# An attention, gated MLP and squared-ReLU MLP kernel: q and k transposed in memory, and a list scheduler in place of a table of times

## The chip, the cores and the metric

The kernel runs on one core of one Trainium2 chip. The metric is the device time of an execution in microseconds, the median of several runs. The five engines have queues of their own, each worked off in order: TensorE (PE; its loads of weights are PEld), VectorE (DVE), ScalarE (ACT), GpSimd (POOL) and SyncE (SP, which here only issues transfers). An instruction that has to wait for another engine holds up all that stands behind it in its queue.

## What is computed

```python
scores = scale * np.matmul(q, k.transpose(0, 1, 3, 2))          # B, H, S, D = 2, 8, 768, 64
is_global = pos[None, :] < int(n_global)                         # 8
is_local = (rel >= 0) & (rel < int(n_local))                     # 96
dist = np.where(is_global & ~is_local, float(n_local), np.abs(rel).astype(np.float32))
scores = scores - slopes[:, None, None] * dist[None, :, :]
scores = np.where(is_global | is_local, scores, -1000000000.0)
a = np.exp(scores - np.max(scores, axis=-1, keepdims=True))
x = np.matmul(a / (np.sum(a, axis=-1, keepdims=True) + 1e-09), v)   # to 1536 tokens x 512
...
xn = x / np.sqrt(np.mean(x * x, axis=-1, keepdims=True) + 1e-06) * rms_g
g = xn @ w_gate                                                  # 512 x 1536
x = g * (1.0 / (1.0 + np.exp(-g))) * (xn @ w_val) @ w_out        # 1536 x 512
...
r = np.maximum(x @ w_in, 0.0)                                    # 512 x 2048
return (s * (r * r) + b) @ w_out2                                # 2048 x 512
```

The weights of the MLPs are 64-bit floating point in memory and are converted in the kernel. All products are of 32-bit numbers split into a high and a low part: hi x hi, lo x hi and hi x lo are added up.

## The kernel before

A first branch (L993) tests that the mask has its known size and takes `fast_program` (L583); the other branch is not run here. A **unit** is a block of 128 queries of one batch; there are 12 (L576), in the order block 0 of both batches, block 1 of both, and so on. A unit sees 232 keys: 8 global ones, 96 before the block and its own 128 (for block 0 only its 128). It has two **groups** of four heads, 24 in all.

For each unit `emit_t` (L655) has PE transpose q and k (`transposes`, L225, recorded at L228) out of tiles that SP loads with 256-byte rows (`load_qk`, L609), splits them from PSUM into high and low parts (L689 to L694, L673, L676) on ScalarE and VectorE, and `shift` (L645, L652) moves the last 96 keys of the block before to the front of the window. `emit_s` (L706) makes the scores of a group (L721); VectorE adds the distances and finds the extreme value (L735), ScalarE makes the exponentials (L750), VectorE the reciprocal of the sums (L760, L761), GpSimd mostly normalizes (L762). `emit_p` transposes the weights (L782), ScalarE or VectorE copies them out of PSUM (L786, L788), `emit_x` multiplies with v (L807). `Mlp.finish` (L375) then norms a unit's 128 tokens: squares on ScalarE, their sum on VectorE (L381), two small products on PE (L384, L391), a power on GpSimd (L388), the scaling on VectorE (L395) and the split into `xyh` and `xyl` (L403 to L407).

An **item** is the gate and value product (24 matmuls) of one of the first four slices f of 128 hidden columns with 256 tokens (`hb`). Items are PE's filler in the attention stage (`gate_val`, L830); where there is none yet, `keep_warm` (L210, L215) puts matmuls without use there. Each weight goes through seven steps (`steps`, L298): magnitude (ScalarE, L304), floor (GpSimd as a rule, L307), shift and two merges (VectorE, L309 to L312), high part (ScalarE, L319), low part (GpSimd as a rule, L321). A ring of eight holds converted weights, three buffers the raw ones.

What orders the attention stage is the table `SCH` (L39): for each kind of step and each group a time, in units of a group, and for some the engine. Every step is put into a heap with its time (`at`, L603) and recorded when its time is the least (L886 to L888). After it `mlp.run` (L446) does the rest: first the items that are left, halves of one slice and 512 tokens together, then the other slices of gate and value, `w_out`, `w_in`, `w_out2`; weights are converted as it goes on.

Of the kernel before, what the change touches and what calls it, by code (L numbers as in the profile page):

```python
# [14 lines left out]
ALU = mybir.AluOpType  # L15
# [15 lines left out]
WIN = GLOB + PREV + 128  # L31
KA = GLOB + PREV
# [6 lines left out]
SCH = {  # L39
    "exp": [0.406, 0.27, -0.303, 0.212, 0.116, 0.271, 0.267, 0.276, 0.13, 0.198, 0.245, -0.017, 0.207, 0.102, 0.226, 0.093,  # L40
     0.229, 0.063, 0.093, 0.104, 0.446, 0.273, 0.395, 0.115],
    "nrm": [0.47, 0.057, 0.226, 0.329, 0.232, 0.292, 0.157, 0.111, -0.107, 0.33, 0.258, 0.244, 0.279, 0.33, 0.325, 0.292, -0.129,
     0.382, 0.399, 0.382, 0.957, 0.22, 0.706, 0.494],
    "nrmV": [1, 0, 0, 0, 0, 0, 0, 0, 0, 0, 1, 0, 0, 0, 0, 0, 0, 0, 0, 0, 0, 0, 0, 0],
    "cp": [[1.578, 1.356, 1.511, 1.695, 1.502, 1.722, 1.62, 1.606, 1.716, 1.318, 1.604, 1.565, 1.357, 1.884, 1.72, 1.721, 1.707,
      1.261, 1.519, 1.48, 2.115, 1.317, 1.296, 1.27],
     [1.809, 1.308, 1.802, 1.667, 1.543, 1.794, 1.284, 1.845, 1.968, 1.901, 1.643, 1.845, 1.845, 2.06, 1.994, 1.88, 2.012,
      1.646, 1.736, 0.894, 1.769, 1.457, 2.015, 0.921]],
    "cpV": [2, 3, 2, 2, 0, 0, 0, 0, 3, 0, 2, 0, 0, 1, 0, 1, 0, 3, 0, 1, 2, 1, 0, 0],
    "gv": [0.52, 0.511, 0.36, 0.367, 0.413, 0.069, 0.482, 0.489, 0.687, 0.535, 0.535, 0.54, 0.449, 0.497, 0.491, 0.465, 0.42,  # L50
     0.413, 0.49, 0.498, 0.644, 0.479, 0.444, 0.451, 0.522, 0.898, 0.79],
    "silu": [0.43, 0.084, -0.119, -0.292, -0.217, -0.528, -0.709, -0.095, -0.138, 0.033, 0.104, -0.177, 0.312, -0.094, 0.03,
     -0.37, 0.197, 0.105, 0.102, -0.062, 0.197, -0.17, 0.097, -0.107, 0.093, 0.07, -0.011],
    "mult": [0.092, 0.611, 0.115, -0.071, -0.311, 0.77, -0.266, 0.298, -0.118, 0.974, 0.112, 0.343, 0.223, 0.14, 0.14, 0.641,
     0.083, 0.654, 0.146, 0.822, 0.076, 0.322, -0.007, 0.811, 0.161, 0.297, -0.14],
    "dum": [4, 6, 5, 3, 0, 0, 0, 3, 7, 7],
    "maxV": [1, 0, 0, 1, 1, 0, 1, 0],
    "loV": [0, 1, 0, 1, 1, 0, 1, 0],
    "T": [-0.692, -1.029, -1.323, -1.024, -1.16, -0.983, -1.043, -0.991, -1.008, -1.263, -0.942, -1.184],
    "shift": [-2.152, -1.955, -2.004, -1.861, -1.935, -1.162, -1.655, -1.947, -1.543, -1.814, -1.669, -1.843],  # L60
    "fin": [[3.268, 3.837, 4.209, 4.21, 4.346, 4.403, 4.976, 4.977], [2.932, 3.306, 4.163, 4.164, 4.27, 4.428, 5.069, 5.12],
# [11 lines left out]
    "conv": [[0.47, 2.049, 2.05, 2.152, 3.896, 3.897], [1.905, 2.353, 3.218, 4.031, 4.064, 4.148],  # L73
# [3 lines left out]
    "mask": -2.172,  # L77
# [7 lines left out]
    "hiV": [0, 1, 0, 0, 0, 0, 0, 0, 0, 0, 0, 1],  # L85
    "shP": [1, 0, 0, 0, 0, 0, 1, 0, 0, 0, 1, 1],
    "top": [-0.042, 0.11, 0.089, 0.074, -0.522, 0.021, 0.095, 0.104, 0.013, -0.261, -0.145, -0.306, -0.167, -0.517, 0.067, 0.202,
     0.062, -0.044, 0.066, -0.509, 0.021, 0.117, 0.141, -0.043],
    "val": [0.768, 0.053, 0.09, -0.108, -0.135, -0.174, 0.09, -0.162, 0.011, -0.109, -0.112, -0.107, -0.234, 0.054, -0.052,
     -0.375, 0.032, 0.166, -0.671, -0.346, -0.661, 0.036, 0.348, 0.117, -0.029, 0.377, -0.348],  # L90
    "fe": [[1, 0], [0, 0], [1, 0], [1, 0], [1, 0], [0, 0], [0, 0], [1, 1], [1, 1], [1, 1], [0, 0], [0, 0]],
    "bmP": [0, 0, 0, 1, 0, 1, 1, 1],
}
SLOPES = [2.0 ** -(h + 1) for h in range(H)]
# [3 lines left out]
def kernel(  # L98
# [34 lines left out]
    nc.sync.dma_start(qn0, q[0, :, 0:128, :].rearrange("h t d -> t h d"))  # L133
    nc.scalar.dma_start(kn0, k[0, :, 0:128, :].rearrange("h t d -> t h d"))


    def distance(Dt, W, base, scr):
# [902 lines left out]
```

## Time and profile before

| | us |
|---|---|
| median of 3 runs | 703.92 (703.17 to 704.7) |
| the profiled execution | 703.05 |
| its span, from first to last instruction | 701.3 |
| PE busy | 672.8 |
| VectorE busy | 436.3 |
| ScalarE busy | 283.5 |
| GpSimd busy | 258.9 |

The span's mean granted TensorE clock is 0.98 of full speed. Busy time counts overlapping instructions of an engine once. A row of the timeline has the start, the time taken and the work; matmuls overlap, so what one costs PE is read from start to start. In the windows each engine's busy time stands in the order PE, PEld, DVE, ACT, POOL.

### The profile page before, as it was taken

The numbers are of one execution on the slowest core, as the hardware profiler recorded it, in microseconds if no ns is written. First come the engines' busy times: TensorE is split into PE (matmuls) and PEld (weight loads), VectorE is DVE, ScalarE is ACT, GpSimd is POOL, SyncE is SP. The second block draws the span as 40 slices with busy tenths as digits, with TensorE's granted clock in tenths as the row PEclk, the third lists the DMA queues.
The fourth block names the chain that finished last, engine by engine and source line by source line (L and its number), as shares of the span: only waits on it lengthen the run. The fifth ranks groups of instructions, "written<-read, shape, count | busy, mean of one in ns | idle before, by whom it ended". The sixth has DMA issues, their size and how long they took to land.

```text
span 701.3 us, 9949 instructions
## 1 busy us (share of the span) xinstructions
PE 672.8 (96%) x3707; PEld 562.6 (80%) x3707; DVE 436.3 (62%) x868; ACT 283.5 (40%) x611; POOL 258.9 (37%) x194
## 2 busy tenths in 40 slices
PE   7789999999999999999999999999999997999996
PEld 5578888989988888887888877888888875888885
DVE  6989897775577766778432379654544599322332
ACT  3766566654233322334332344433333454322321
POOL 1644454333356654566200066433333377000000
PEclk7869999999999999999999999999999999999999
DMA  7754543410032331223200023221122222100101
GB/s 169 160 118 114 120 103 76 99 45 1 8 114 90 93 117 61 91 90 108 75 0 1 0 88 120 66 89 60 61 64 80 68 92 89 61 1 0 61 1 65
DMA packets 64562, 51.11 MB, mean 73 GB/s; under 512 B 29624, under 2 KB 59384, under 8 KB 64504
## 3 DMA queue, kind: packets, MB, share of 16 engines
q1 hardware_dynamic: 63320, 50.11, 25.2%
q8 instruction: 31, 0.51, 0.3%
q10 hardware_dynamic: 1184, 0.26, 0.2%
q14 instruction: 27, 0.22, 0.1%
HBM read 47.22 MB, written 3.15 MB: 72 GB/s over the span
## 4 chain that ended last, share of the span: by engine, by line
PE 82%; DVE 6%; POOL 4%; ACT 3%; DMA 2%; issue 2%; SPq 0%; POOLq 0%; ACTq 0%; DVEq 0%
PE ps L223 24%; PE ps L222 24%; PE ps L221 24%; PE ps L782 2%; PE ps L807 2%; PE ps L721 2%; PE ps L228 1%; DMA raw_p<-in_moe_w_out_dram 1%; POOL u L307 1%; ACT t L750 1%; DMA side<-in_q_dram 1%; DVE u L309 1%; DVE u L310 1%; PE ps L391 1%; POOL t L762 1%
## 5 line engine op out<-in xcount | busy, mean ns | idle before, releaser
L307 POOL TENSOR_SCALAR u<-u 128x512 f32<-128x512 f32 x64 | 111.2, 1738 | 143.4 <-ACT u L304 143.4
L221 PE MATMUL ps<-xyh,hi_i 128*128 128x512 f32 x192 | 74.7, 389 | 0.0
L222 PE MATMUL ps<-xyl,hi_i 128*128 128x512 f32 x192 | 74.7, 389 | 0.0
L223 PE MATMUL ps<-xyh,lo_i 128*128 128x512 f32 x192 | 74.7, 389 | 0.0
L514 DVE SCALAR_TENSOR_TENSOR gt<-side,sb 128x512 f32<-128x512 f32 x48 | 38.5, 803 | 57.3 <-ACT side L513 57.3
L221 PE MATMUL ps<-xyh,hi_g 128*128 128x512 f32 (+1 forms) x188 | 65.3, 347 | 0.0
L221 PE MATMUL ps<-xyh,hi_v 128*128 128x512 f32 (+1 forms) x188 | 64.0, 340 | 0.0
L222 PE MATMUL ps<-xyl,hi_v 128*128 128x512 f32 (+1 forms) x188 | 63.8, 339 | 0.0
L223 PE MATMUL ps<-xyh,lo_v 128*128 128x512 f32 (+1 forms) x188 | 63.8, 339 | 0.0
L222 PE MATMUL ps<-xyl,hi_g 128*128 128x512 f32 (+1 forms) x188 | 63.7, 339 | 0.0
L223 PE MATMUL ps<-xyh,lo_g 128*128 128x512 f32 (+1 forms) x188 | 63.7, 339 | 0.0
L309 DVE TENSOR_SCALAR u<-u 128x512 int32<-128x512 int32 x68 | 61.4, 903 | 2.2 <-POOL u L307 2.1
L513 ACT ACTIVATE side<-ps 128x512 f32<-128x512 f32 x48 | 28.7, 598 | 76.7 <-PE ps L223 76.7
L762 POOL TENSOR_TENSOR t<-t,sm 128x928 f32<-128x928 f32 (+1 forms) x22 | 36.7, 1670 | 59.1 <-ACT xn L379 20.9
L428 ACT ACTIVATE side<-ps 128x512 f32<-128x512 f32 (+1 forms) x47 | 23.3, 497 | 86.5 <-PE ps L223 86.3
L750 ACT ACTIVATE t<-t,mn 128x232 f32<-128x232 f32 (+1 forms) x96 | 44.2, 463 | 16.0 <-DVE mn L735 15.9
L222 PEld LDWEIGHTS ps<-xyl,hi_i 128*128 128x128 f32 x192 | 36.0, 188 | 7.5
L223 PEld LDWEIGHTS ps<-xyh,lo_i 128*128 128x128 f32 x192 | 36.0, 188 | 7.5
L434 DVE TENSOR_TENSOR p<-side,ps 128x512 f32<-128x512 f32 (+1 forms) x47 | 26.3, 560 | 25.2 <-PE ps L223 24.9
L221 PEld LDWEIGHTS ps<-xyh,hi_i 128*128 128x128 f32 x192 | 36.0, 188 | 7.3
L429 DVE SCALAR_TENSOR_TENSOR side<-side,ps 128x512 f32<-128x512 f32 (+1 forms) x47 | 26.3, 559 | 23.7 <-ACT side L428 23.6
L223 PE MATMUL ps<-hi_p,ev 128*128 128x512 f32 x96 | 37.8, 394 | 2.5 <-DVE ev L521 2.5
(155 smaller groups left out, 1650.1 us busy)
## 6 DMA issues: line engine op xcount, KB each, us to landing
raw_i<-in_moe_w_in_dram SPq DMA_DIRECT2D x16, 512.0 KB, 4.0
raw_p<-in_moe_w_out_dram SPq DMA_DIRECT2D x16, 512.0 KB, 3.2
raw_g<-in_moe_w_gate_dram SPq DMA_DIRECT2D x12, 512.0 KB, 3.5
raw_v<-in_moe_w_val_dram SPq DMA_DIRECT2D x12, 512.0 KB
raw_o<-in_moe_w_out_dram SPq DMA_DIRECT2D x12, 512.0 KB, 3.3
vw<-in_v_dram SPq DMA_DIRECT2D x10, 448.0 KB, 4.4
out_dram<-o SPq DMA_DIRECT2D x12, 256.0 KB, 2.1
qn<-in_q_dram SPq DMA_DIRECT2D x11, 256.0 KB, 3.9
```

What stands on the lines that cost most here:

```text
L221: T.matmul(out=o, lhsT=ahi, rhs=bhi, start=first, stop=False)
L222: T.matmul(out=o, lhsT=ahi, rhs=blo, start=False, stop=False)
L223: T.matmul(out=o, lhsT=alo, rhs=bhi, start=False, stop=last)
L307: eng[0].tensor_scalar(u, u, 2.0**-15, None, op0=ALU.max)
L309: V.tensor_scalar(ui, ui, 5, 2, op0=ALU.logical_shift_left, op1=ALU.logical_shift_right)
L428: A.activation(th[:, :w], g, AF.Tanh, scale=0.5)
L429: V.scalar_tensor_tensor(th[:, :w], in0=th[:, :w], scalar=1.0, in1=g, op0=ALU.add, op1=ALU.mult)
L434: yield lambda: V.tensor_tensor(pt[:, c0:c1], th[:, :w], vv, op=ALU.mult)
L513: A.activation(r, o, AF.Relu)
L514: V.scalar_tensor_tensor(g, in0=r, scalar=s_col, in1=r, op0=ALU.mult, op1=ALU.mult)
L750: A.activation(t[:, hh, :W], t[:, hh, :W], AF.Exp, bias=mn[:, hh : hh + 1], scale=-1.0, accum_out=sm[:, hh : hh + 1],)
L762: (V if SCH["nrmV"][gi] else P).tensor_tensor(t[:, :, :W], t[:, :, :W], sm.unsqueeze(2).to_broadcast([128, 4, W]), op=ALU.mult)
```

## The change

1. The host lays q and k out with the head dimension first, so a unit's q is a plain 128 x 512 load. k and v have the 8 global keys ahead of every block; a block of k has 136 columns. The transposes on PE and the moves of old keys go. A split of k writes 136 columns (232 in three units, where the key buffer starts anew) behind the block before in a buffer of three blocks; the window is a view of 232 columns of it, in the order 96 earlier, 8 global, 128 own.
2. The scores are scaled in the step that adds the distances, and their PSUM tile is one of two banks; so is that of the transposed weights, which one copy empties.
3. Units go through batch 0 and then batch 1, after block 0 of both.
4. `SCH` goes. Every step is an `Op` with its possible engines and assumed durations, what it comes after, and what buffers it takes and gives; `arrange` takes the one that can start first, by rank among those that start within `LOOK`, and the list is recorded by start time. The row sums of squares may go to GpSimd (two adds), as may the subtractions of q and k, which have no PSUM operand now. Items that it would start after the last unit's norm are left to `mlp.run`.
5. In `mlp.run` the floor of a weight is VectorE's.

```diff
-    qn0, kn0 = (t.rearrange("p (h d) -> p h d", h=H) for t in side[:2])
+    q0, k0 = (t.rearrange("p (a c) -> p a c", a=NPAIR) for t in side[:2])
...
+    banks = {"a": (0, 1, 2, 3), "gv": (4, 5, 6, 7), "x": (0, 1), "u": (2, 3), "w": (6, 7), "xx": (8,), "yy": (9,)}
...
-    def transposes(nat):
...
+        def steps(self, key):
+            magnitude, floor, shifts, low, high, hi_part, lo_part = self.stages(key)
+            magnitude(A)
             yield 0
-            eng[0].tensor_scalar(u, u, 2.0**-15, None, op0=ALU.max)
+            floor(V)
             yield 1
...
+            def add(e):
+                if e is P:
+                    P.tensor_tensor(xn[:, 0:2], xn[:, 0:2], xn[:, 2:4], op=ALU.add)
+                    P.tensor_tensor(ss, xn[:, 0], xn[:, 1], op=ALU.add)
+                    return
+                V.tensor_reduce(out=ss, in_=xn.rearrange("p a c -> p c a"), op=ALU.add, axis=AX.X)
...
-    units = [(b, i) for i in range(NT) for b in range(B)]
+    units = [(b, 0) for b in range(B)] + [(b, i) for b in range(B) for i in range(1, NT)]
...
+    def arrange(ops, size):
...
+        while left:
+            cands = []
+            for op in left:
...
+                _, d, e, t = min((max(t, free[e]) + d + SPARE.get(e, 0.0), d, e, max(t, free[e])) for e, d in op.on.items())
+                cands.append((t, op, d, e))
+            t0, _, _, e = min(cands, key=lambda c: (c[0], c[1].rank))
+            t0, op, d, e = min((c for c in cands if c[3] == e and c[0] <= t0 + LOOK.get(e, 0.0)), key=lambda c: c[1].rank)
+            op.start, op.end, op.eng = t0, t0 + d, e
...
+        return sorted(done, key=lambda o: o.start)
...
+                loads[n] = op("wload", -3 + 0.1 * n, lambda e: mlp.load(), {"S": 0.9}, take=["raw"])
...
+            for m, on in enumerate(({"V": 0.45}, {"V": 0.5}, {"V": 0.7}, {"V": 0.7}, {"A": 0.64}, {"V": 0.72, "P": 1.45}), 1):
...
+                    st["q"] = in_p.tile([128, NPAIR, 128], F32, name="q", tag="q")
+                    nc.sync.dma_start(st["q"], q[b, i])
...
+            def q_lo(e, st=st):
+                e.tensor_tensor(st["ql"], st["q"], st["qh"].bitcast(F32), op=ALU.subtract)
...
+            def k_lo(e, st=st):
+                hi, lo = st["kd"]
+                e.tensor_tensor(lo, st["k"], hi.bitcast(F32), op=ALU.subtract)
...
+            ql = op("split", r - 1.5, q_lo, {"V": 0.72, "P": 1.35}, [qh], give=[("qraw", lq)])
...
+                nr = op("nrm", rg, normalise, {"V": 0.72, "P": 1.3} if first else {"P": 1.9, "V": 1.15}, [iv])
...
+        items = [(f, hb) for hb in range(B * S // HB - 1) for f in range(G0)]
...
+        end = max(o.end for o in xs)
+        late = {o.item for o in plan if o.item and o.kind == "gate" and o.start > end} - {
+            o.item for o in plan if o.item and o.kind == "gate" and o.start <= end
+        }
+        done |= {o.item for o in plan if o.item} - late
+        for o in plan:
+            if o.item in late:
+                continue
+            if o.eng == "T":
+                if o.start < COLD and o.start - free > 0.6 and not live:
+                    keep_warm(int((o.start - free - 0.3) / 0.25))
+                free = o.end
...
+            o.fn(engines[o.eng])
...
+        if name == "q":
+
+            a = a.reshape(B, NPAIR, 2, NT, 128, D).transpose(0, 3, 2, 5, 1, 4).reshape(B, NT, 128, NPAIR, 128)
```

Three places show how the order of the instructions changes. The first is PE's queue in the filled part of the attention stage (`ps` are PSUM tiles; `kwh`, `kwl` and `kw` parts of k, `qhi`, `qlo` of q, `t` the exponentials, `pt` their transposes, `vw` v). Before, from the last scores of a group on:

```order
L721 MATMUL ps_925<-kwl_199,qhi 128x232
L721 MATMUL ps_926<-kwl_199,qhi 128x232
L228 MATMUL ps_948<-ident,qn 128x128 x4
L228 MATMUL ps_960<-ident,kn 128x128 x4
L807 MATMUL ps_862<-pt,vw 64x128 x8
L782 MATMUL ps_991<-ident,t 116x128 x4
L782 MATMUL ps_997<-ident,t 116x128 x4
L215 MATMUL ps_1003<-warm 128x512 x7
```

And now, at a like place:

```order
L182 MATMUL ps_1169<-xyh,hi_v 128x256
L183 MATMUL ps_1169<-xyl,hi_v 128x256
L184 MATMUL ps_1169<-xyh,lo_v 128x256
L377 MATMUL ps_1215<-ones,ss 128x1
L884 MATMUL ps_1227<-pt,vw 64x128 x8
L810 MATMUL ps_1241<-kw_1103,qhi 128x232 x2
L810 MATMUL ps_1241<-kw_1103,qlo 128x232 x2
L810 MATMUL ps_1241<-kw_1104,qhi 128x232 x2
```

The transposes (L228) and the warming matmuls are gone, and matmuls of an item stand in halves between the steps of attention. Before the first item stand eight score groups before and eleven now.

The second is GpSimd's queue early in the attention stage. Before, from the second of its normalizations (`bm` are the distances times slopes, `u` and `lo_g` a weight in conversion, `xyl` a unit's low part):

```order
L762 TENSOR_TENSOR t<-t,sm 128x4x128
L307 TENSOR_SCALAR u<-u 128x512
L762 TENSOR_TENSOR t<-t,sm 128x4x128
L307 TENSOR_SCALAR u<-u 128x512
L321 TENSOR_TENSOR lo_g<-u,hi_g 128x512
L388 TENSOR_TENSOR rstd<-rstd,mhalf 128x1
L762 TENSOR_TENSOR t<-t,sm 128x928
L407 TENSOR_TENSOR xyl<-xn,xyh 128x4x128
```

And now, from the low part of the third unit's k:

```order
L787 TENSOR_TENSOR kw_215<-k,kw_214 128x4x136
L764 TENSOR_TENSOR qlo<-q,qhi 128x512
L370 TENSOR_TENSOR xn<-xn 128x256
L371 TENSOR_TENSOR ss<-xn 128x128
L849 TENSOR_TENSOR t<-t,sm 128x4x128
L384 TENSOR_TENSOR rstd<-rstd,mhalf 128x1
L849 TENSOR_TENSOR t<-t,sm 128x4x128
L764 TENSOR_TENSOR qlo<-q,qhi 128x512
```

The floors (L307) have left GpSimd; the subtractions of q and k (L764, L787) and the sums of squares (L370, L371) have come to it.

The third is SP's queue behind the branch. Before:

```order
L614 DMA qn<-in_q_dram 128x8x64
L615 DMA kn<-in_k_dram 128x8x64
L623 DMA vw<-in_v_dram 128x8x64
L282 DMA raw_g<-in_moe_w_gate_dram 128x4x256
L623 DMA vw<-in_v_dram 128x8x64
L282 DMA raw_v<-in_moe_w_val_dram 128x4x256
L282 DMA raw_g<-in_moe_w_gate_dram 128x4x256
```

And now:

```order
L237 DMA raw_g<-in_moe_w_gate_dram 128x4x256
L237 DMA raw_v<-in_moe_w_val_dram 128x4x256
L237 DMA raw_g<-in_moe_w_gate_dram 128x4x256
L737 DMA k<-in_k_dram 128x4x128
L751 DMA vw<-in_v_dram 128x512 x2
L723 DMA q<-in_q_dram 128x512
```

The three weight loads (512 KB each) stand ahead of the second unit's k, v and q (256 KB each), where they stood behind its q and k.

## Rows read from the trace of the kernel before

**Rows 1.** The page, part 1: busy us, share of the span, instructions of an engine.

```profile
PE 672.8 (96%) x3707; PEld 562.6 (80%) x3707; DVE 436.3 (62%) x868; ACT 283.5 (40%) x611; POOL 258.9 (37%) x194
```

**Rows 2.** Windows: busy us of PE, PEld, DVE, ACT, POOL; clock; DMA; GB/s.

```profile
11.00:62.47 51.47, 43.09 (x320) 36.00 (x319) 45.42 (x152) 33.29 (x105) 24.70 (x23) 0.77 0.67 161
62.47:181.44 118.97, 114.72 (x1115) 104.45 (x1113) 90.62 (x299) 67.87 (x205) 49.12 (x41) 1.00 0.30 69
181.44:700.00 518.56, 508.40 (x2258) 417.24 (x2256) 293.75 (x387) 179.69 (x298) 183.58 (x120) 1.00 0.20 65
```

**Rows 3.** The chain of waits near 135 us: start, us, work.

```profile
134.31 0.87 PE ps L721 x12
135.17 1.02 PE ps L228 x8
136.20 1.02 PE ps L807 x16
137.22 1.07 PE ps L782 x8
```

**Rows 4.** Timeline: start, us, work; first transposes, third scores, first product, later ones, two tanh.

```profile
7.74 0.45 PE L228 MATMUL ps<-ident,side 128*128 128x128 f32 x1 [2.71 <-DMA side<-in_q_dram]
...
20.93 0.45 PE L721 MATMUL ps<-kwh,qhi 64*128 64x128 f32 x2
...
62.47 0.37 PE L221 MATMUL ps<-xyh,hi_g 128*128 128x256 f32 x1
...
178.56 0.28 PE L221 MATMUL ps<-xyh,hi_g 128*128 128x256 f32 x1
...
181.44 0.28 PE L221 MATMUL ps<-xyh,hi_g 128*128 128x256 f32 x1
...
225.66 0.60 ACT L428 ACTIVATE side<-ps 128x512 f32<-128x512 f32 x1 [2.85 <-PE ps L223]
...
231.10 0.60 ACT L428 ACTIVATE side<-ps 128x512 f32<-128x512 f32 x1 [2.85 <-PE ps L223]
```

**Rows 5.** Groups by shape, VectorE, 11 to 62.47 us: busy, mean ns, idle before.

```profile
L310 DVE SCALAR_TENSOR_TENSOR u<-raw_g,u 128x512 int32<-128x512 int32 x3 | 3.6, 1214 | 0.1
L676 DVE TENSOR_TENSOR kwl<-ps,kwh 128x512 fp32r<-128x512 f32 x5 | 3.4, 684 | 0.2 <-ACT kwh L673 0.2
L381 DVE TENSOR_REDUCE ss<-xn 128x128 f32<-128x512 f32 x3 | 3.1, 1045 | 0.0
...
L694 DVE SCALAR_TENSOR_TENSOR qlo<-ps,qhi 128x512 fp32r<-128x512 f32 x4 | 2.7, 684 | 0.0
...
L652 DVE CAST kwl<-kwl 128x384 fp32r<-128x384 f32 x3 | 2.1, 704 | 0.0
...
L310 DVE SCALAR_TENSOR_TENSOR u<-raw_v,u 128x512 int32<-128x512 int32 x2 | 1.4, 692 | 0.1
```

**Rows 6.** The same of GpSimd.

```profile
L762 POOL TENSOR_TENSOR t<-t,sm 128x928 f32<-128x928 f32 x4 | 6.9, 1733 | 4.9 <-DVE sm L761 2.4 <-ACT pt L788 2.4
...
L407 POOL TENSOR_TENSOR xyl<-xn,xyh 128x512 fp32r<-128x512 f32 x2 | 2.6, 1280 | 5.2 <-DVE xyh L403 4.0 <-PE ps L228 1.2
L388 POOL TENSOR_TENSOR rstd<-rstd,mhalf 128x1 f32<-128x1 f32 x3 | 1.8, 595 | 3.9 <-DVE rstd L387 2.9 <-DVE sm L760 1.0
```

**Rows 7.** Timeline near 229 us, then line 309: ns min/median/max.

```profile
228.90 1.28 POOL L321 TENSOR_TENSOR lo_v<-u,hi_v 128x512 fp32r<-128x512 f32 x1
...
228.99 1.48 DVE L309 TENSOR_SCALAR u<-u 128x512 int32<-128x512 int32 x1
...
L309 DVE TENSOR_SCALAR u<-u x68: 397/454/1518, 21.6 to 591.4; 128x512 int32<-128x512 int32 x68
```

**Rows 8.** Windows, with columns as in rows 2: start, gate stage, last conversions.

```profile
8.00:18.00 10.00, 9.28 (x47) 7.63 (x47) 7.45 (x32) 4.35 (x13) 1.43 (x4) 0.50 1.06 259
200.00:260.00 60.00, 60.00 (x267) 49.69 (x266) 44.87 (x56) 19.08 (x32) 35.79 (x22) 1.00 0.32 97
560.00:600.00 40.00, 35.91 (x147) 26.25 (x146) 35.17 (x40) 18.64 (x30) 28.52 (x19) 1.00 0.24 81
```

More of the change, by code (lines that the diff above doesn't have):

```diff
@@ L295, in place, with stages @@
             return self.ring
-        def steps(self, key, eng=(P, P)):
+        def stages(self, key):
             kind, f = key
@@ new lines, in high, with hi_part @@
+            def high(e):
+                V.scalar_tensor_tensor(ui, in0=h32, scalar=-1073741824, in1=ui, op0=ALU.bitwise_and, op1=ALU.bitwise_or)
+                if self.loaded < len(self.seq):
+                    self.load()
+            def hi_part(e):
+                pool = self.place(kind, f)
+                part["hi"] = pool.tile([128, 512], F32R, name=f"hi_{kind}", tag="hi")
+                part["lo"] = pool.tile([128, 512], F32R, name=f"lo_{kind}", tag="lo")
+                part["ring"] = pool is self.ring
+                A.activation(part["hi"], u, AF.Copy)
@@ new lines, in lo_part @@
+            def lo_part(e):
+                hi, lo = part["hi"], part["lo"]
+                e.tensor_tensor(lo, u, hi.bitcast(F32), op=ALU.subtract)
+                if kind in "gvi":
+                    hi, lo = (t.rearrange("p (k c) -> p k c", k=KD) for t in (hi, lo))
+                self.w[key] = (hi, lo, part["ring"])
+            return magnitude, floor, shifts, low, high, hi_part, lo_part
+        def steps(self, key):
+            magnitude, floor, shifts, low, high, hi_part, lo_part = self.stages(key)
+            magnitude(A)
@@ new lines, in total, with mean, root, spread @@
+            def total(e):
+                part["R"] = ps("w")
+                T.matmul(out=part["R"][:, 128:129], lhsT=ss, rhs=ones, start=True, stop=True)
+            def mean(e):
+                part["r"] = nrm.tile([128, 1], F32, name="rstd", tag="rstd")
+                V.tensor_scalar(part["r"], part["R"][:, 128:129], 1.0 / DM, 1.0e-6, op0=ALU.mult, op1=ALU.add)
+            def root(e):
+                P.tensor_tensor(part["r"], part["r"], mhalf, op=ALU.pow)
+            def spread(e):
+                T.matmul(out=part["R"][:, :128], lhsT=part["r"].to_broadcast([128, 128]), rhs=ident, start=True, stop=True)
@@ L581, with __init__ @@
     nc.sync.dma_start(sb[:, 1:2], b2.partition_broadcast(128))
+    class Op:
+        def __init__(self, kind, rank, fn, on, after=(), take=(), give=()):
+            self.kind, self.fn, self.on, self.after, self.take, self.give = kind, fn, on, after, take, give
+            self.rank = rank + AHEAD.get(kind, 0.0)
+            self.item = None
+            self.start = self.end = self.eng = None
+    def arrange(ops, size):
+        free = dict.fromkeys("PVATS", 0.0)
+        takes = {r: [] for r in size}
+        gives = {}
+        left, done = list(ops), []
+        while left:
+            cands = []
+            for op in left:
+                t = 0.0
+                for a in op.after:
+                    a, lag = a if isinstance(a, tuple) else (a, 0.0)
+                    if a.end is None:
+                        t = None
+                        break
+                    t = max(t, a.end + lag + (0.3 if a.eng == "T" else 0.08))
+                if t is None:
+                    continue
+                for r in op.take:
+                    n = len(takes[r]) - size[r]
+                    if n >= 0:
+                        if (r, takes[r][n]) not in gives:
+                            t = None
+                            break
+                        t = max(t, gives[r, takes[r][n]] + 0.1)
+                if t is None:
+                    continue
+                _, d, e, t = min((max(t, free[e]) + d + SPARE.get(e, 0.0), d, e, max(t, free[e])) for e, d in op.on.items())
[3 more added lines that the diff above has]
+            op.start, op.end, op.eng = t0, t0 + d, e
+            end = op.end
+            free[e] = end
+            for r in op.take:
+                takes[r].append(op)
+            for g in op.give:
+                gives[g] = end
+            left.remove(op)
+            done.append(op)
+        return sorted(done, key=lambda o: o.start)
     def fast_program(fctx):
@@ new lines, in fast_program, with op, bm0_half @@
+        engines = {"P": P, "V": V, "A": A, "T": T, "S": nc.sync}
+        size = {"xx": 1, "u": 2, "yy": 1, "w": 2, "qraw": 1, "kraw": 1, "v": 2, "qs": 2, "kw": 1, "kf": 1, "t": 3, "pt": 2}
+        size |= {"nr": 2, "cv": 3, "raw": 3, "th": 2}
+        ops = []
+        def op(kind, rank, fn, on, after=(), take=(), give=()):
+            ops.append(Op(kind, rank, fn, on, after, take, give))
+            return ops[-1]
+        def bm0_half(e):
+            for h in range(4):
+                V.tensor_scalar(bm0[1][:, h, :], D0, -8.0 * SLOPES[4 + h], None, op0=ALU.mult)
```

678 lines of the change are left out of this document (322 added, 356 removed), and 21 rows, old and new, of the table SCH.

## Prediction

> **What bounds the kernel now.** I read the page's engine shares first: TensorE (PE) is busy 96% of the span, VectorE 62%, GpSimd 37% [rows 1]. An average over stages does not say where a microsecond can be won, so next come three windows [rows 2], cut at two instructions of the timeline [rows 4]: the first gate product at 62.47 us, and 181.44 us, where the table's last product of the attention stage ends and the MLP's own loop begins.
>
> In the first window (the **opening**) VectorE is busy 45.42 of 51.47 us, and PE runs at a mean clock of 0.77: PE has warming matmuls and no other filler, and VectorE's queue sets the pace. In the second (the **filled stretch**) PE is busy 114.72 of 118.97 us at full clock; the products fill what attention leaves, so an instruction taken off PE there ends the stretch earlier. In the third PE is busy 508.40 of 518.56 us; it is the MLP and the change leaves its matmuls alone.
>
> The chain of waits gives PE's price of each piece in the filled stretch, start to start [rows 3]: a group's scores 0.87 us, the eight transposes of a unit's q and k 1.02, weights times values 1.02, transposes of the weights 1.07. A gate-and-value item of 256 columns is 181.44 less 178.56, or 2.88 us, and one of 512 columns is the distance of two tanh, 5.44 us [rows 4].
>
> **The sum.** I write the new span as opening E, plus filled stretch, plus the rest.
>
> *Filled stretch before, to test the prices.* From the order of PE's instructions, after the first product stand 19 items (54.7 us), 16 score groups (13.9), 17 groups of transposed weights (18.2), 18 products with v (18.4), the q and k transposes of 7 units (7.1) and 7 warming matmuls (7 x 5.44/24 = 1.6): 113.9 us. The stretch lasted 118.97; the 5.1 us left are two small products for each of ten units and the idle time.
>
> *Filled stretch after.* The new order has 12 items (34.6), 13 score groups (11.3), 16 of transposed weights (17.1), 17 products with v (17.3), no q and k transposes and no warming: 80.3. With the same 5.1 it lasts 85.4 us.
>
> *Rest.* The scheduler leaves out every item whose products it would start after the last unit's normalization, so the MLP's loop has 4 items of 256 columns and 4 of 512 at its start (33.3 us) where it had 3 and 1 (14.1). The rest was 701.3 - 181.44 = 519.9 and becomes 539.1. Moving items costs and gains nothing in the sum, since the filled stretch lost them.
>
> So the span is E + 624.5 + x, with x for new stalls in the filled stretch, and the change is faster if E + x stays under 76.8. Before, E was 62.5.
>
> *E: the start.* The q and k transposes leave the head of PE's queue; they waited 2.71 us for a transfer and started at 7.74 [rows 4]. But SP now issues three weight loads ahead of the second unit's k, v and q. Up to that q it is 3 x 512 + 4 x 256 KB, 2.6 MB; at the 259 GB/s that the queues moved then [rows 8] that is 10 us, so q is there at about 17.8. A split on ScalarE or VectorE (0.6 to 0.7, by the 128x384 cast of rows 5) and a subtraction on GpSimd (1.28, by L407 [rows 6]) put the third score group at about 20 us; before, it was at 20.93. The transposes saved at the start are thus given back: the gain begins after this group.
>
> *E: VectorE.* The window to the first product loses on VectorE the subtractions of k and q from PSUM (3.4 and 2.7), the moves of old keys (2.1 for the low halves and about as much for the high) and the row sums (3.1) [rows 5], together 13.4 us. By the new order three weights are converted by then where five were; the four VectorE steps of one take 0.4 to 1.2 us each, so some 6 us go. Put back are four casts of q and five subtractions of parts of q, k and x: 0.64 at least (the cast of 384 columns), 1.3 at most (GpSimd's price for 512), I take 0.8, 7 us. That leaves about 33 of 45.4 us. At the same busy share, 88%, that is 37.5 us and E = 48.5.
>
> *E: GpSimd.* Between the third score group and the first product its queue holds eight subtractions of 512 or 544 columns (1.28 each), four normalizations of 928 columns (1.73), two of 512 (about 1.28), two powers (0.6) and three pairs of adds that stand for VectorE's row sum; an add of 256 or 128 columns lies between 0.6 (one column) and 1.28 (512), I take 0.85, so 5.1 us [rows 6]. That is 26 us, so the product cannot start before about 46; at 80% busy it is 52.5. Where it was 48% busy, GpSimd now ends waits as often as VectorE. I take **E = 54**. The floor is 47, both queues without a gap; the upper end is 60, GpSimd at 65%.
>
> *x.* VectorE has less to do in the filled stretch too, but GpSimd has the subtractions and sums, in 85 us and not 119. An engine that was busy 49.12 of 118.97 us comes to some 70%, and three engines at 70 to 80% with queues in a fixed order do not always meet PE's need. PE idled 4.25 us with the old table; I take x = 4, with 0 (PE still the slowest, the others run ahead) and 12 (a tenth of the old stretch) as ends.
>
> *The MLP's conversions.* The floor of each weight moves from GpSimd to VectorE, for some 52 weights. In the gate stage VectorE is busy 44.87 of 60 us and PE never idles [rows 8]: an added 0.45 us (the median of the shift of the same size [rows 7]) per 5.44 us has room. Only in the burst of 560 to 600 us is VectorE nearly full, and PE lost 4.1 of 40 us there [rows 8]. The floors are also taken out of the queue of the engine that VectorE's shifts waited for, so I cost this at 0, between -4 (the idle time goes) and +5 (eight floors of 0.6 on the full engine).
>
> The distances' three pieces, the global keys that now come with each block (136 columns, not 128), one copy of both banks of transposed weights in place of two: all lie under the above, and are worth under 1 us each on PE. Fewer, longer rows in the transfers matter only at the start, where the weight loads hide it.
>
> Sum: 54 + 85.4 + 4 + 539.1 = **682.5 us** of span, 18.8 less than 701.3. The profiled run took 703.05, in line with the median 703.92, so the median comes to **685 us**.
>
> **A rule that speaks against it.** Next to GpSimd's lo_v at 228.90 us, VectorE's shift of 128x512 takes 1.48 us; its shortest is 0.397 and the median 0.454 [rows 7]. One merge takes 1.214 us in the mean in the opening, its twin 0.692 [rows 5]. So VectorE waits for GpSimd here, about 0.5 to 1.1 us each time. The Trainium skill (SBUF — State Buffer, "Who interferes with whom") says the two engines share a port pair under an exclusive lock, and that a VectorE instruction with two SBUF inputs also contends with one of GpSimd that reads SBUF. The trace agrees as far as the merges go. By it the subtractions that read PSUM and one SBUF tile, and now read two SBUF tiles, become open to this wait.
>
> **Rivals.**
> *GpSimd in the way.* Some 24 of VectorE's instructions in the opening read SBUF alone; if a quarter of GpSimd's instructions each cost one of them 1 us, E goes to 60, and x to 12: 60 + 85.4 + 12 + 539.1 = 696.5, so 699 for the median. For it: the waits just told, and GpSimd's share. Against: before, PE idled in spite of them only 4.25 us.
> *Nothing in the way.* E = 48, x = 1: 673.5, so 676. For it: by engine sums VectorE and GpSimd could be through by then. Against: the old opening was at 88% and not 100.
> *Weights late, slower than before.* At the first product five of eight ring weights are still to be converted, where three were; the new order asks for them within the 12 items, and PE's queue cannot pass an item whose weight is not there. Each step of a conversion stands in VectorE's queue behind score groups. If each of the five comes 2 to 3 us late, x is 13; with E = 64 the sum is 701.5 and over, I put it at 704, so **707**. It decides from E + x = 76.8. Against it: the conversion is some 5 us of work in a stretch of 85.
> *It does not do what it says.* The order has no q or k transpose left and q comes as rows of 512 elements, so this is out.
>
> **Chances.** Forecast (676 to 694) 0.59; nothing in the way 0.09; GpSimd in the way (692 to 701) 0.20; weights late 0.12. Under 676 lies most of the second, over 700 the last: the range is **676 to 700**. A measurement of this kernel tells about 0.2%, 1.4 us, from no change: faster 0.85 (all but 0.03 of the third case), same 0.03, slower 0.12.
>
> **What would show it.** The first gate product between 47 and 60 us; the stretch from there to the MLP's loop near 89 us with PE over 92% busy; the third score group near 20 us; no PE wait for lo or hi of a gate weight; PE idle between the last conversions unchanged. A first product after 62 us, or PE idle over 16 us in the filled stretch, makes the prediction wrong; PE losing over 9 us in the last conversions would mean that the floor's move is what mattered.

## The result: 707.98 us, slower than before, and the profile after

The change takes 707.98 us in the median (706.88 to 712.22), the kernel before 704.41 in the same comparison: a ratio of 1.0061, 95% interval 1.0043 to 1.0080. The forecast was 685, the range 676 to 700.

In the page of the changed kernel, part 1, TensorE lost 9.5 us of work against [rows 1] and two points of its share, for a span 4.7 us longer:

```profile
PE 663.3 (94%) x3558; PEld 549.5 (78%) x3558; DVE 436.5 (62%) x879; ACT 286.2 (41%) x599; POOL 183.3 (26%) x153
```

Its windows, with the columns of [rows 2], cut at the same two instructions: the first gate product, at 60.80 us, and the first product of the MLP's loop, at 167.88.

```profile
11.00:60.80 49.80, 36.83 (x308) 28.23 (x306) 40.49 (x142) 32.43 (x105) 27.70 (x24) 0.86 0.51 151
60.80:167.88 107.08, 91.77 (x885) 82.02 (x883) 81.78 (x253) 69.33 (x190) 70.58 (x59) 0.94 0.31 90
167.88:706.00 538.12, 527.49 (x2352) 433.81 (x2352) 308.07 (x454) 181.82 (x302) 82.27 (x60) 1.00 0.21 62
```

Against the forecast span (54 + 85.4 + 4 + 539.1 = 682.5) the opening is 6.8 us longer, the filled stretch 17.7 (107.1 for 89.4), and the rest 1.0 shorter: 706.0. So x is 21.7 and not 4. Of it 11.1 us are idle time: PE idles 15.3 us of the stretch, where it idled 4.25 [rows 2]. The other 10.6 us are busy time: PE is busy 91.8 us, where the forecast stretch less its idle time is 85.4 - 4.25, or 81.2. Part of the busy time is the clock, 0.94 and no longer 1.00.

PE's waits up to the MLP's loop are led by one line, the products with v (L884) waiting for ScalarE's copy of the transposed weights (L872). Two single waits, of 6.0 us before 38.7 and of 6.1 before 99.3, make nearly all of it; the first lies in the opening, the second in the filled stretch. The second one, in the chain of waits (start, us, work):

```profile
87.90 9.25 DMA q<-in_q_dram
97.17 0.63 ACT qhi L761
97.80 0.52 ACT xyh L409
98.32 0.92 ACT pt L872
99.28 1.98 PE ps L884 x16
```

The copy takes 0.92 us. It is late because it stands behind the cast of the *next* unit's q in ScalarE's queue, and that cast waits for its load. In ScalarE's timeline the queue stands still for 7.7 us, while the transposed weights have been in PSUM since 90.9:

```profile
88.78 0.67 ACT L262 ACTIVATE u<-raw_v 128x512 f32<-128x512 f32 x1
97.17 0.63 ACT L761 ACTIVATE qhi<-q 128x512 fp32r<-128x512 f32 x1 [7.72 <-DMA q<-in_q_dram]
97.71 0.61 ACT L409 ACTIVATE xyh<-xn 128x512 fp32r<-128x512 f32 x1
98.23 1.00 ACT L872 ACTIVATE pt<-ps 116x1024 f32<-116x1024 f32 x1
```

Why the load is late stands in SP's queue. q's 256 KB are issued behind a weight (512 KB) and v (464 KB), all at once, and take 9.25 us; the last q load, behind one weight only, takes 4.12.

```profile
86.91 0.39 SPq L237 DMA_DIRECT2D raw_g<-in_moe_w_gate_dram  x1
87.39 0.41 SPq L751 DMA_DIRECT2D vw<-in_v_dram  x1
87.90 0.41 SPq L723 DMA_DIRECT2D q<-in_q_dram  x1
88.41 0.55 SPq L737 DMA_DIRECT2D k<-in_k_dram  x1
```

The kernel before did the reverse. After a unit's transposes (L228) its table issued the next q first; the next transposes came some 12 us later (79.40), and after the opening no engine there waited for a q or k load at all:

```profile
67.06 0.39 SPq L614 DMA_DIRECT2D qn<-in_q_dram  x1
67.55 0.52 SPq L615 DMA_DIRECT2D kn<-in_k_dram  x1
68.56 0.38 SPq L628 DMA_DIRECT2D vw<-in_v_dram  x1
68.99 0.33 SPq L629 DMA_DIRECT2D vw<-in_v_dram  x1
73.81 0.38 SPq L282 DMA_DIRECT2D raw_g<-in_moe_w_gate_dram  x1
```

The clock multiplies the stall. In the changed kernel's windows of 5 us (busy times, granted clock, DMA), PE falls idle at 92 us, and when its work comes it runs at half rate (1.2 GHz): the products with v take 1.98 us and not 1.02.

```profile
90.00:95.00 5.00, 2.04 (x16) 1.75 (x15) 4.97 (x20) 0.00 (x0) 1.50 (x1) 1.00 0.61 162
95.00:100.00 5.00, 0.72 (x8) 0.72 (x10) 0.58 (x2) 2.83 (x7) 2.12 (x2) 0.65 0.11 38
100.00:105.00 5.00, 5.00 (x40) 4.47 (x38) 1.80 (x10) 2.93 (x12) 5.00 (x5) 0.66 0.54 161
```

The clock is low in one other place of the stretch, from 70.87 to about 77 us, behind a wait of 2.03 us that is not ScalarE's; the experiment without the add comes back to it. PE's busy time times the missing share of the clock, summed over windows of 5 us, makes 4.7 us in the stretch: 2.8 there and 1.9 behind the stall at 99.28.

A second trouble shows on VectorE, which is busy 81.8 us of the stretch. One tiny add, of 1e-9 to four row sums a partition, is stretched to up to ten times its length, where in the kernel before it never was. Changed kernel, then before: ns min/median/max.

```profile
L844 DVE TENSOR_SCALAR sm<-sm x24: 153/170/1723, 15.9 to 150.5; 128x4 f32<-128x4 f32 x24
```

```profile
L760 DVE TENSOR_SCALAR sm<-sm x24: 153/169/171, 14.3 to 165.4; 128x4 f32<-128x4 f32 x24
```

The two timelines side by side say what stretches it. Of the 24 adds of the changed kernel 11 take over 0.2 us. Each of these begins while GpSimd is inside a subtraction, a normalization or an add, and ends 0.02 to 0.03 us after that instruction does. Of the other 13 one meets GpSimd at work (at a power of one column), and of the 24 in the kernel before none does. The longest, in the changed kernel:

```profile
79.19 1.74 POOL L849 TENSOR_TENSOR t<-t,sm 128x928 f32<-128x928 f32 x1 [1.80 <-ACT t L838]
79.23 1.72 DVE L844 TENSOR_SCALAR sm<-sm 128x4 f32<-128x4 f32 x1 [0.26 <-ACT t L838]
80.99 0.18 DVE L845 RECIPROCAL sm<-sm 128x4 f32<-128x4 f32 x1
```

### The profile page after: what moved, and what is told of

Its sections match the earlier page's. It is cut to its first block, busy times and chain, and to the rows that moved or that the text cites. A ratio compares the mean times of both kernels' runs of the same rounds, so it can differ in the third digit from the quotient of the medians.

```text
span 706.0 us, 9562 instructions
## 1 busy us (share of the span) xinstructions
PE 663.3 (94%) x3558; PEld 549.5 (78%) x3558; DVE 436.5 (62%) x879; ACT 286.2 (41%) x599; POOL 183.3 (26%) x153
## 4 chain that ended last, share of the span: by engine, by line
PE 78%; DVE 9%; DMA 6%; ACT 2%; issue 2%; POOL 1%; SPq 1%; ACTq 0%; DVEq 0%; POOLq 0%
PE ps L182 24%; PE ps L184 24%; PE ps L183 24%; DMA q<-in_q_dram 5%; PE ps L884 2%; DVE u L269 2%; DVE u L275 2%; PE ps L810 1%; PE ps L865 1%; DVE t L823 1%; DVE u L272 1%; DMA words<-in_n_local_dram 1%; DVE sm L844 1%; DVE u L266 1%; ACT t L838 1%
## 5 line engine op out<-in xcount | busy, mean ns | idle before, releaser
L182 PE MATMUL ps<-xyh,hi_g 128*128 128x512 f32 (+1 forms) x176 | 63.0, 358 | 0.9 <-DVE p L949 0.9
L184 PE MATMUL ps<-xyh,lo_v 128*128 128x512 f32 (+1 forms) x176 | 61.6, 350 | 0.0
L184 PE MATMUL ps<-xyh,lo_g 128*128 128x512 f32 (+1 forms) x176 | 61.6, 350 | 0.0
L288 POOL TENSOR_TENSOR lo_i<-u,hi_i 128x512 fp32r<-128x512 f32 x16 | 23.3, 1455 | 138.9 <-ACT hi_i L284 137.5
L435 ACT ACTIVATE side<-ps 128x512 f32<-128x512 f32 (+1 forms) x32 | 18.3, 571 | 95.8 <-PE ps L184 95.8
L269 DVE TENSOR_SCALAR u<-u 128x512 int32<-128x512 int32 x68 | 51.2, 753 | 0.0
L436 DVE SCALAR_TENSOR_TENSOR side<-side,ps 128x512 f32<-128x512 f32 (+1 forms) x32 | 20.9, 654 | 42.8 <-ACT side L435 42.8
L266 DVE TENSOR_SCALAR u<-u 128x512 f32<-128x512 f32 x68 | 40.2, 593 | 4.6 <-ACT u L262 4.5
L884 PE MATMUL ps<-pt,vw 116*64 116x128 f32 (+1 forms) x352 | 27.2, 300 | 14.8 <-ACT pt L872 12.5
L288 POOL TENSOR_TENSOR lo_p<-u,hi_p 128x512 fp32r<-128x512 f32 x16 | 22.0, 1377 | 72.4 <-ACT hi_p L284 67.6
```

The source lines that it names most:

```text
L182: T.matmul(out=o, lhsT=ahi, rhs=bhi, start=first, stop=False)
L184: T.matmul(out=o, lhsT=alo, rhs=bhi, start=False, stop=last)
L266: e.tensor_scalar(u, u, 2.0**-15, None, op0=ALU.max)
L269: V.tensor_scalar(ui, ui, 5, 2, op0=ALU.logical_shift_left, op1=ALU.logical_shift_right)
L288: e.tensor_tensor(lo, u, hi.bitcast(F32), op=ALU.subtract)
L435: A.activation(th[:, :w], g, AF.Tanh, scale=0.5)
```

## Experiments

In the expectations, theory **Q** is the late load of q, **G** GpSimd and VectorE in each other's way, **V** VectorE with too much work, **O** an order that is poor whatever the loads do. Every ratio is to the kernel before, with its 95% interval. "The order" is the order of the instructions that the list gave.

**Is it the loads of q? One q for all.**

```diff
-                    st["q"] = in_p.tile([128, NPAIR, 128], F32, name="q", tag="q")
-                    nc.sync.dma_start(st["q"], q[b, i])
+                    if not same:
+                        same["q"] = in_p.tile([128, NPAIR, 128], F32, name="q", tag="q")
+                        nc.sync.dma_start(same["q"], q[b, i])
+                    st["q"] = same["q"]
```

> All units after the first use the q of the second unit: ten of the eleven q loads are left out, with the order of every other instruction as in the change. Theory Q (q's load comes late: it has one buffer, stands in SP's queue behind k, v and weight loads, and its cast then holds ScalarE's queue): the two long PE waits of the change (6.0 us at 32.7 and 6.1 us at 93.1) and the low clock behind them go, the filled stretch falls from 107 to 88 to 95 us, time 685 to 697. Rival G (GpSimd and VectorE in each other's way): within 3 us of the change, 704 to 711. Rival O (the list's order is poor whatever the loads do): PE's long waits stay at other instructions, 701 to 710.

692.93 us, 0.9833 (0.9815 to 0.9850): 15 us under the change with the same order of work on the four compute engines. Theory Q. Both 6 us waits are gone and the first product comes at 56.84. But the stretch still takes 99.9 us, longer than Q had said, and the low clock, which Q had said would go, stays:

```profile
56.84:156.75 99.91, 91.22 (x885) 82.03 (x883) 82.92 (x253) 69.69 (x190) 71.47 (x58) 0.95 0.28 83
```

PE's idle time falls from 15.3 to 8.7 us, its busy time from 91.8 to 91.2 only, and low clock still costs 4.7 us of it. So the late q is most of the new idle time, and something else is in the rest.

**Two buffers for q, the order as it was.**

```diff
-                    st["q"] = in_p.tile([128, NPAIR, 128], F32, name="q", tag="q")
+                    st["q"] = q_odd if n % 2 else in_p.tile([128, NPAIR, 128], F32, name="q", tag="q")
```

> q gets a second buffer (odd units use a tile of the first activation's pool), the order is that of the change, so SP issues the same loads in the same order and only q's wait for the subtraction before it is gone. Theory Q, if the single buffer is most of it: 685 to 698, SP's wait of L723 on the subtraction under 5 us in all. Theory Q, if the place in SP's queue behind weight and v loads is most of it: 700 to 707. Rivals G and O: 704 to 711.

710.12 us, 1.0084 (1.0067 to 1.0101), no better; the number alone lies with G and O. Near the same place of SP's queue the q load is issued at the same time as before, to 0.02 us, because the queue's head is the weight load, waiting for *its* buffer:

```profile
86.92 0.39 SPq L237 DMA_DIRECT2D raw_g<-in_moe_w_gate_dram  x1
87.41 0.42 SPq L752 DMA_DIRECT2D vw<-in_v_dram  x1
87.88 0.45 SPq L724 DMA_DIRECT2D q<-in_q_dram  x1
```

**Two buffers, and q first in SP's queue.** After the list is made, each q load is moved right behind the subtraction that frees its buffer.

```diff
+        for n in range(2, NU):
+            o = lqs[n]
+            plan.remove(o)
+            plan.insert(1 + max(plan.index(lqs[n - 1]), plan.index(qls[n - 2])), o)
```

> Two q buffers as in the run before, and each q load is issued on SP right behind the subtraction that frees its buffer, ahead of the v and weight loads that stood before it; the same loads, and the order of the other engines as in the change. If the place in SP's queue is the cause: ScalarE's and VectorE's waits for q fall from 15 and 5 us to under 3, 690 to 698, near the run with one q (692.9). If the transfers are what is slow (1.2 to 1.5 MB under way at a time), q is still late: 702 to 710.

698.96 us, 0.9925 (0.9908 to 0.9942), a whole kernel that beats both, 1 us above what was said for the place in the queue. The same place again: q goes out 0.9 us ahead of the weight, and its cast runs at 85.45 without a wait, so it landed within 3.4 us.

```profile
82.01 0.36 SPq L725 DMA_DIRECT2D q<-in_q_dram  x1
82.96 0.40 SPq L237 DMA_DIRECT2D raw_g<-in_moe_w_gate_dram  x1
83.44 0.36 SPq L753 DMA_DIRECT2D vw<-in_v_dram  x1
84.33 0.55 SPq L739 DMA_DIRECT2D k<-in_k_dram  x1
```

So, given the second buffer, the place in the queue was the cause, and the buffer alone was not; q first with one buffer was not tried. VectorE's and ScalarE's waits for q fall from 20.6 us to 2.7; k is now the late one (ScalarE waits 7.8 us for it); that this is part of the 6 us to the run with one q is not shown.

**What the list believes of a load.**

```diff
-                lag = 2.2
+                lag = 7.0
```

> The list is told that a q or k load takes 7.0 us in place of 2.2; buffers and operations as in the change, the order is another. Theory Q: the list puts the casts of q and k behind the copies of the transposed weights and fills the time with products: PE's wait for pt falls from 12.5 us to under 5, time 688 to 701. Rival G: 703 to 712. Rival O: anything, but PE waits of over 5 us in one piece stay.

701.21 us, 0.9951 (0.9933 to 0.9969): one number in the scheduler's costs, 6.8 us, and 0.2 us outside Q's range. No PE wait for pt remains among its long ones. Together with q first:

> The list made with 7.0 us for a load (701.2 us with one buffer), and two q buffers with the q loads ahead in SP's queue. Theory Q, if late loads still cost in that run: 692 to 699. If the list with 7.0 us has already covered them: 699 to 703, no gain.

700.45 us, 0.9936 (0.9913 to 0.9960), not told apart from 701.21: the list with 7.0 has already covered the loads. A list with two buffers and 5.0 us:

> The list knows of two q buffers and counts 5.0 us for a load, and the second product with v of a unit is tied behind the first. Theory Q: the list then issues q about a unit earlier and puts the casts where the loads have landed: 688 to 699, PE's wait for pt under 4 us. Rival O (the list's order is poor whatever the loads do): 700 to 710.

704.56 us, 0.9997 (0.9986 to 1.0007). Q's number was missed. Its wait for pt did fall, to 3.3 us, but PE waits 5.6 us for the low halves of k and the first product comes at 62.71. Another order brings other waits; on this run O was right.

**Is the rest v's load?** The first kernel leaves out nine loads of v on top of the one-q run; the second is whole: three buffers of v, and q, k and v all issued as soon as their buffers are free.

> As the run with one q, and the v of the third unit serves all units after it, so nine of the v loads are left out too; the order of the other engines as in the change. Theory Q with v: PE's issue waits at the products with v (3.0 us in the run with one q, 3.6 in the one with q loads first) are v's load, and go: 686 to 691. If they are something else: 691 to 695. What is then left over the forecast of 685 is not a matter of loads.

> Nothing is left out: two buffers of q and three of v (the added ones lie in the first activation's pool, which the attention stage uses in part), and q, k and v loads each issued right behind the instruction that frees the buffer; the weight loads come after them; the other engines' order as in the change. Theory Q with v: 689 to 697, below the 699.0 with q first alone, and no issue wait of over 1 us at a product with v. If the transfers share one rate and something is always late: 697 to 704.

694.91 us, 0.9875 (0.9857 to 0.9893), and 698.18, 0.9908 (0.9891 to 0.9925): no gain over 692.93 and 698.96. That idea fell. The second run also issues k earlier: ScalarE's waits for k fall from 7.8 us to 4.6, and the time stays where it was. In the run with three v buffers the products with v still wait 3.66 us, until 69.53, and its VectorE timeline says for what: for the scaling (L398) that frees their PSUM bank (in the run with one v the profile names it as what ends this wait), and this stands behind an add of four numbers a partition that takes 1.29 us, while GpSimd subtracts for 2.14 (second fence).

```profile
65.87 1.12 DVE L864 TENSOR_TENSOR t<-t,sm 128x928 f32<-128x928 f32 x1
66.91 1.29 DVE L859 TENSOR_SCALAR sm<-sm 128x4 f32<-128x4 f32 x1
68.24 0.18 DVE L860 RECIPROCAL sm<-sm 128x4 f32<-128x4 f32 x1
68.33 1.09 DVE L398 SCALAR_TENSOR_TENSOR xn<-ps,gcol,ss 128x128 f32<-128x128 f32 x4
```

```profile
66.03 2.14 POOL L797 TENSOR_TENSOR kw<-k,kw 128x544 fp32r<-128x544 f32 x1 [2.42 <-DVE kw L791]
```

**VectorE's work, or GpSimd's hold on it?** Six runs move work between the two at the same places of the order: the subtractions of q and k to VectorE (in the change; with q first; with one q), the normalizations to VectorE (with one q), the floors of the eight weights of this stage to GpSimd (in the change; with three v buffers). The edits are all of this form:

```diff
-                e.tensor_tensor(st["ql"], st["q"], st["qh"].bitcast(F32), op=ALU.subtract)
+                V.tensor_tensor(st["ql"], st["q"], st["qh"].bitcast(F32), op=ALU.subtract)
```

> All subtractions that make the low halves of q and k run on VectorE, at the places that the list gave them; the order on PE, ScalarE and SP is the same. Rival G: GpSimd's share of the stretch falls and VectorE's stretched instructions with it, time 695 to 704. Theory Q: the stalls at q's loads stay, 704 to 712; slower by up to 4 us, since VectorE is at 76% in the stretch.

> The floor of the eight weights that are converted in the attention stage runs on GpSimd, as all but a few did in the kernel before, at the place that the list gave it; the loop of the MLP keeps it on VectorE. Theory V (with q on time VectorE, busy all of 80 to 125 us in the run with one q, is the second limit, and the floors, 0.4 to 1.5 us each, are part of it): with q as late as in the change 3 to 8 us of VectorE's work go, but the stalls at q's loads stay: 700 to 706. Theory Q alone: 704 to 710, since VectorE isn't what PE waits for. Rival G (GpSimd in the way): 707 to 716, by eight more GpSimd instructions of about 1.7 us.

> The kernel before this one in the list, and the floors of the eight weights of the attention stage on GpSimd. Theory V (with the loads on time VectorE is what PE waits for): 2 to 6 us less than that one. Rival G: 1 to 6 us more, by GpSimd's eight floors of about 1.7 us.

> The run with q loads first (699.0 us), and all subtractions of q and k on VectorE at the same places: 17 instructions leave GpSimd (1.3 to 2.0 us each) for VectorE (0.7 to 1.1 each). Theory V (VectorE has too much work): 701 to 708. Rival G (GpSimd holds VectorE): VectorE's other instructions get shorter by as much as the added ones cost, 694 to 699.

> The run with one q for all units but the first (692.9 us), and the subtractions of q and k on VectorE as in the run before this. Theory V: 695 to 702. Rival G: 687 to 692, and the mean of the add on the row sums (0.54 us there) falls toward 0.17.

> The run with one q, and all normalizations on VectorE at the same places: 13 of them leave GpSimd's filled stretch (26.1 us there, 2.0 each) for VectorE (1.1 each, 15 us), which is 83% busy in it. Theory V: 700 to 712. Rival G, if holding is the larger cost: 687 to 693; a mixture: 694 to 699.

| moved | us | ratio | without the move |
|---|---|---|---|
| subtractions to VectorE, change | 707.58 | 1.0047 (1.0033 to 1.0062) | 707.98 |
| the same, q first | 699.06 | 0.9931 (0.9909 to 0.9954) | 698.96 |
| the same, one q | 696.48 | 0.9894 (0.9877 to 0.9910) | 692.93 |
| normalizations to VectorE, one q | 695.23 | 0.9865 (0.9839 to 0.9890) | 692.93 |
| floors to GpSimd, change | 706.36 | 1.0035 (1.0017 to 1.0054) | 707.98 |
| floors to GpSimd, three v buffers | 699.05 | 0.9917 (0.9897 to 0.9937) | 698.18 |

No move changes the time by more than 3.6 us, and only the one-q subtractions are told apart from the run beside them. Neither V nor G alone fits. By the ranges, the two moves in the change are Q's; the subtractions are V's with one q and lie between V and G with q first; the normalizations are the mixture's; the floors with three v buffers are neither's. The add's mean, which G said would fall toward 0.17 us when the subtractions leave GpSimd, falls from 0.47 to 0.41 with one q and from 0.55 to 0.35 with q first: GpSimd's other instructions still hold it. The windows of one q and of its run with the normalizations moved say why (busy PE, PEld, DVE, ACT, POOL):

```profile
11.00:157.00 146.00, 131.36 (x1192) 113.06 (x1191) 124.29 (x394) 102.05 (x293) 99.83 (x81) 0.94 0.33 100
```

```profile
11.00:157.00 146.00, 129.66 (x1186) 111.09 (x1187) 126.61 (x413) 102.05 (x293) 63.81 (x62) 0.92 0.33 100
```

VectorE took over 19 normalizations; its normalizations went from 6.4 to 26.2 us in the groups by shape of the two runs, yet its busy time rose by 2.3. Its other instructions got 17.5 us shorter when GpSimd lost 36.0 us of work. So by these records some 17.5 of VectorE's 124.3 "busy" us are waiting inside its instructions, and what a move takes off one engine it puts on the other: the time did not fall.

**Take a held instruction away.** The run with q first without the add on the row sums:

```diff
-                    V.tensor_scalar(sm, sm, 1.0e-9, None, op0=ALU.add)
                     V.reciprocal(sm, sm)
```

> The run with q loads first (699.0 us) without the add of 1e-9 to the row sums: every sum holds an exp of 0 and is at least 1, so the add changes nothing in float32. 24 VectorE instructions go, 13.2 us in that run's records (0.55 us each; 0.17 unhindered). Theory V (the recorded time is VectorE's work): 690 to 696. Rival G (GpSimd's instruction holds whatever comes next): the reciprocal takes over the waiting, its mean goes from 0.18 to about 0.5 us, 697 to 700.

693.48 us, 0.9851 (0.9834 to 0.9867): the **best whole kernel** here, 5.5 us under q first. The time is in V's range (690 to 696). G as I had put it, a hold that passes to whatever comes next (697 to 700), is out: the reciprocal did not take over the waiting. In the run's groups by shape it stays at 170 ns, where the run with the add had 551 for the add and 178:

```profile
L848 DVE RECIPROCAL sm<-sm 128x4 f32<-128x4 f32 x24 | 4.1, 170 | 1.6 <-ACT t L842 1.5
```

```profile
L848 DVE TENSOR_SCALAR sm<-sm 128x4 f32<-128x4 f32 x24 | 13.2, 551 | 0.7 <-ACT t L842 0.5
L849 DVE RECIPROCAL sm<-sm 128x4 f32<-128x4 f32 x24 | 4.3, 178 | 0.8
```

The same edit in the change and in the kernel before:

> The change without the add of 1e-9 to the row sums (12.1 us of VectorE's records up to 160 us, 0.50 us each), everything else as in the change. If GpSimd's hold on VectorE is the second half of the miss: 700 to 705, 3 to 8 us under the change. If the late q loads cover it: 706 to 709.

> The kernel before without the same add (24 of 0.17 us, never over 0.171). If the gain of 5.5 us came from the hold: within 1.4 us of the kernel before, 702 to 705. If the add costs in any order: 697 to 702.

702.63 us, 0.9975 (0.9957 to 0.9992), and 702.26, 0.9973 (0.9964 to 0.9983). It gives 5.4 us in the change and 1.6 in the kernel before (4.0 us of adds there, none held), which is inside G's 702 to 705, if at its edge. So 1.6 us is what the add costs in the kernel before, where nothing holds it, and the other 3.8 of the 5.4 go with the hold.

Where the hold reached PE in the change is the wait before 70.87 us. The products with v waited for the scaling (L398) that frees their bank, and this stood behind an add of 1.33 us; then the clock fell. Without the add the same products wait 0.42 us and the clock stays up, while the stall of the late q, 7.3 us in that run, is still there. Changed kernel, then without the add (rows of the timelines, then a window of 5 us):

```profile
68.22 1.33 DVE L844 TENSOR_SCALAR sm<-sm 128x4 f32<-128x4 f32 x1
69.67 1.10 DVE L398 SCALAR_TENSOR_TENSOR xn<-ps,gcol,ss 128x128 f32<-128x128 f32 x4
70.87 1.98 PE L884 MATMUL ps<-pt,vw 116*64 116x128 f32 x16 [2.03 <-issue]
70.00:75.00 5.00, 4.13 (x26) 3.49 (x28) 3.30 (x14) 3.91 (x12) 3.82 (x4) 0.50 0.44 117
```

```profile
69.12 1.09 PE L883 MATMUL ps<-pt,vw 116*64 116x128 f32 x16 [0.42 <-ACT pt L871]
70.00:75.00 5.00, 5.00 (x56) 4.26 (x52) 5.00 (x17) 4.45 (x17) 3.99 (x4) 1.00 0.43 118
```

**The floors of the MLP's loop back on GpSimd.**

```diff
-                e.tensor_scalar(u, u, 2.0**-15, None, op0=ALU.max)
+                (e if self.plan else P).tensor_scalar(u, u, 2.0**-15, None, op0=ALU.max)
```

> The change with the floors of the MLP's own loop back on GpSimd, those of the attention stage on VectorE. The prediction costed the move of these floors at 0, between a gain of 4 and a loss of 5 us. If so: 706 to 710, within 2 us of the change (708.0). If VectorE was made the loop's limit: under 704. If GpSimd's floors held up the loop before: 711 to 714.

710.15 us, 1.0085 (1.0064 to 1.0107), not told apart from 1.0061: the move was worth 0, perhaps 2 us gained.

## Why the prediction was wrong

*What held.* The third score group came at 19.76 us (said: near 20). The rest is 538.1 us (said: 539.1). The floors cost nothing. No PE wait for a gate weight shows, so the rival "weights late", whose 707 us is nearly the result, had the number and not the mechanism: late were q's loads, because of the weights' place in SP's queue.

*The step that failed* is "x", the 4 us of new stalls, which came to 21.7, and with it the 54 us of "E", which came to 60.8. I worked both from the shares of VectorE and GpSimd alone. Of the loads I said that they "matter only at the start, where the weight loads hide it". But the change takes away what separated the load from its users. Before, a q was freed by PE's transposes and needed about 12 us later; now its buffer is held to the end of the subtraction, the load is issued behind a weight and v, and the cast that needs it stands in ScalarE's queue ahead of the copies for which PE waits. I counted the bytes ahead of q for the first 20 us only. SP's order puts a weight, a v and a q together for two later units (issued by 27.8 and by 87.9 us), and the scheduler counts 2.2 us for a load that took 6.6 to 9.6 us behind others; both were there to be read. With q on time, 15.05 of the 23 us of the miss go (692.93 for 707.98): in the profiled runs, of which that with one q was 3.4 us above its median, 4.0 us of the opening and 7.2 of the stretch, nearly all of it idle time of PE.

*The second step* is the rival "GpSimd in the way", which I gave 0.20. I had its row (the shift of 1.48 us [rows 7]) and its mechanism, and argued against it that PE had idled only 4.25 us in spite of it. My "0.5 to 1.1 us each time" took 0.5 from a mean of three merges; one of them had taken 2.26 us, the others 0.69. In the new order GpSimd is busy 70.6 of 107 us, where it was 49.1 of 119 [rows 2], so more of VectorE's short instructions meet it, in the chain to PE. The add alone is worth 5.4 us in the change, 3.8 of them by the hold; the 0.33 us between its mean of 0.503 and 0.170, over 24 adds, are 8 us of VectorE. The Trainium skill (SBUF — State Buffer, "Who interferes with whom") lists copies, casts and tensor_scalar among the operations that can take the shared port pair, under a lock for the whole instruction. The trace agrees: the add, a tensor_scalar, and a cast of q (1.88 us in the one-q run, 0.43 in the median of the change) are stretched, and the reciprocal, which the page does not list, stays at 177 to 180 ns in the change and with q first, also where it falls wholly inside an instruction of GpSimd (8 times in the change). I had weighed that page for operations with two inputs in SBUF, and not for these.

*A smaller one.* The 12 items were priced whole, at 2.88 us. The new list cuts them into 29 pieces; read from start to start the pieces take 39.0 us in place of 34.6, and as much in the run with q first and no add, where the clock of the stretch was 0.98.

*What stays open.* 15.05 and 5.35 are 20.4 of 23 us, if they add up (5.5 us also came with q first, where the late loads were gone); one q and no add together was not run. The clock's part I did not try by itself. Of the 4.7 us that low clock costs in the stretch, 2.8 stand behind the held add and 1.9 behind the late q; with one q it is still 4.7. So of the 10.6 us of new busy time the late q explains little; the low clock and the cut items, 4.4 us, are read from the trace. That k holds the kernel with q first is not shown: in the run that issues k earlier nothing was gained.

## What to carry to other kernels

When a change takes a step out between a load and its user, price the load again, for every repetition and not only the first: where it stands in its queue, what it waits behind, how long it takes in company, and what stands behind its first user in that engine's queue. In a scheduler's table the assumed time of a load is as much a part of the order as the ranks; here one number was worth 6.8 us. And when an engine looks full, look at the minimum and maximum of its short instructions before counting its busy time as work.

## What had not been expected of the hardware

Moving 19 normalizations, 36 us of GpSimd's time, to VectorE raised VectorE's busy time by 2.3 us. A 128x4 add took from 0.15 to 1.72 us beside GpSimd's work, while the 128x4 reciprocal right behind it never left 0.18; the held adds ended 0.02 to 0.03 us after the instruction of GpSimd beside which they began. And 256 KB that landed within 3.4 us with q first in the queue took 9.25 behind 976 KB issued within a microsecond.
